# Linear-attention queries sketched like keys, and the token routing moved into a scatter under the attention

## The chip, the cores and the metric

The kernel runs on one core of a Trainium2 chip. The metric is device time in microseconds (us) of one execution; lower is better. TensorE (PE) multiplies matrices into PSUM, VectorE (DVE) and ScalarE (ACT) read PSUM and SBUF, GpSimd (POOL) here does a few elementwise operations and issues the indirect DMAs, SyncE (SP) issues the direct ones. Each engine runs its own instructions in order.

## The reference

```python
# attention: q, k, v are (4, 4, 1088, 32), S1 and S2 are (8, 32)
def phi(x):
    a = np.einsum('rd,bhsd->bhsr', S1, x)
    b = np.einsum('rd,bhsd->bhsr', S2, x)
    return np.einsum('bhsi,bhsj->bhsij', a, b).reshape(*x.shape[:-1], r * r)
q_p, k_p = (phi(q), phi(k))
kv = np.einsum('bhsf,bhsd->bhfd', k_p, v)
z = np.sum(k_p, axis=2)
num = np.einsum('bhsf,bhfd->bhsd', q_p, kv)
den = np.einsum('bhsf,bhf->bhs', q_p, z)[..., None] + 1e-06
x = (num / den)                      # then (B, H, S, D) -> (B*S, H*D) = (4352, 128)
# router over E = 8 experts, one expert for each token
xn = x / (np.linalg.norm(x, axis=-1, keepdims=True) + 1e-06)
en = expert_emb / (np.linalg.norm(expert_emb, axis=-1, keepdims=True) + 1e-06)
logits = xn @ en.T / tau
expert_idx = np.argmax(logits, axis=1)
gate_w = probs[np.arange(N), expert_idx]           # probs: softmax of logits over the experts
for e in range(E):
    mask = expert_idx == e
    h = np.maximum(x[mask] @ w1[e], 0.0)               # w1[e] is 128 x 1024
    out[mask] = gate_w[mask, None] * (h @ w2[e])       # w2[e] is 1024 x 128
```

All arrays are float32 (S1 and S2 arrive as 64-bit words).

## The kernel before

The four batches are handled as two halves `m` (2176 tokens each, 17 columns of 128 tokens). Keys of a half go through `k_steps` in groups of four columns: `tr` transposes four tiles on TensorE, `ab` multiplies them with the block matrix `Sblk` (96 columns wide) to get both sketches of all heads, VectorE forms the 64 products of each head (L276), and `kv` accumulates features times `[v, v, 1]` for pairs of heads (L288, 128 outputs by 96 columns, of which the cross terms are masked away with `maskh`).

Queries (`q_steps`) run otherwise. After the transposes, `fa` and `fb` multiply the transposed group with `Sa` and `Sb`, which repeat each sketch row eight times, so that the 64 features of a head come out already transposed (L328, two matmuls of 512 columns each); ScalarE copies one (L335), VectorE multiplies the two (L340). `nd` gives numerator and denominator (L348), with the 64 tokens of each batch written to their own half of the PSUM partitions; VectorE divides (L354 to L356). `xt` transposes x again, ScalarE sums squares (L367), and `logit` multiplies with the normalized expert rows, padded to 96 columns (L372).

The order of steps is given by ticks: `put(tick, steps)` lays the steps of one group on consecutive ticks, and the second half's keys share ticks with the first half's queries. Up to there the framework's scheduler may still reorder; `route_and_run_experts` alone is under a manual schedule of VectorE and TensorE.

Routing begins when all logits are there. `pick` finds the expert of each token, two matmuls (L418, L419) count and rank tokens, `gate_tokens` takes the norm with GpSimd's power (L399), multiplies x by the gate (L408, GpSimd) and stores x to `x_dram` (L410). VectorE then works out each token's slot in a list of 41 blocks of 128 tokens (each block has one expert), builds one-hot rows (L462 to L466), and 34 small matmuls (L469) invert the list into token numbers `src_i` and `dst_i` and an expert number for each block.

The expert loop runs 41 blocks. `fetch(i)` gathers 128 rows of x by an indirect DMA (four blocks ahead), `turn(i)` transposes them, `weights(i)` copies the expert's w1 and w2 with VectorE by a register, `up(i)` is eight matmuls and a Relu on ScalarE, `down(i)` is eight matmuls, a copy on ScalarE and an indirect DMA that scatters the rows to `out`.

Of the kernel before, what the change touches and what calls it, by code (L numbers as in the profile page):

```python
# [19 lines left out]
P = 128  # L20
B, H, S, D = 4, 4, 1088, 32
R = 8
# [11 lines left out]
K_GROUPS = ((0, 4), (4, 8), (8, 12), (12, 16), (16, 17))  # L34
Q_GROUPS = ((0, 4), (4, 8), (8, 11), (11, 14), (14, 17))
# [3 lines left out]
NOWHERE = 8192.0  # L39
DIGIT = 128  # L40
# [9 lines left out]
def kernel(  # L50
# [28 lines left out]
    def ps_acc(i):  # L79
        return psum.tile([P, 512], F32, tag=f"acc{i}", bufs=1, name=f"ps_acc{i}")  # L80
# [6 lines left out]
    def rows_tile(name):  # L87
        return rows_p.tile([P, NC, H, D], F32, tag="rows", name=name)

    def load_q(m):  # L90

        for i in range(2):
            for h in range(H):
                nc.sync.dma_start(
                    q_sb[m][i * HALF:(i + 1) * HALF, :, h],
                    bass.AP(tensor=q.tensor, offset=q.offset + ((2 * m + i) * H + h) * S * D,
                            ap=[[NC * D, HALF], [D, NC], [1, D]]))


    v_sb = [consts.tile([P, 6, NC, D], F32, name=f"v{m}") for m in range(NM)]  # L100

    def load_k(m, i):
        for h in range(H):
            nc.sync.dma_start(
                k_sb[m][:, i * NK:(i + 1) * NK, h],
                bass.AP(tensor=k.tensor, offset=k.offset + ((2 * m + i) * H + h) * S * D,
                        ap=[[NK * D, P], [D, NK], [1, D]]))

    def load_v(m, i):
        for p in range(2):  # L110
            nc.sync.dma_start(
                v_sb[m][:, 3 * p:3 * p + 2, i * NK:(i + 1) * NK],
                bass.AP(tensor=v.tensor, offset=v.offset + ((2 * m + i) * H + 2 * p) * S * D,
                        ap=[[NK * D, P], [S * D, 2], [1, NK * D]]))

    def load_rest(m):
        for i in range(2):
            r = slice(i * HALF, (i + 1) * HALF)
            at = (2 * m + i) * H * S * D + SK * D
            nc.sync.dma_start(k_sb[m][r, NC - 1],  # L120
                              bass.AP(tensor=k.tensor, offset=k.offset + at, ap=[[D, HALF], [S * D, H], [1, D]]))
            for p in range(2):
                nc.sync.dma_start(v_sb[m][r, 3 * p:3 * p + 2, NC - 1],
                                  bass.AP(tensor=v.tensor, offset=v.offset + at + 2 * p * S * D,
                                          ap=[[D, HALF], [S * D, 2], [1, D]]))
# [4 lines left out]
    for m in range(NM):  # L130
        k_sb[m] = rows_tile(f"k{m}")
# [4 lines left out]
        q_sb[m] = rows_tile(f"q{m}")  # L136
# [13 lines left out]
    for m in range(NM):  # L150
        for p in range(2):
            nc.gpsimd.memset(v_sb[m][:, 3 * p + 2], 1.0)

    mask4 = consts.tile([P, H], F32, name="mask4")
    maskh = consts.tile([P, 2], F32, name="maskh")
    for t in (mask4, maskh):
        nc.vector.memset(t, 0.0)
    for h in range(H):
        nc.vector.memset(mask4[h * D:(h + 1) * D, h:h + 1], 1.0)
    for h in range(2):  # L160
        nc.vector.memset(maskh[HALF * h:HALF * (h + 1), h:h + 1], 1.0)
# [28 lines left out]
    nc.vector.tensor_copy(ST, ps[:, :2 * R])  # L190

    Sblk = consts.tile([P, 6, 2 * R], F32, name="Sblk")
    nc.vector.memset(Sblk, 0.0)
    nc.vector.tensor_mul(Sblk[:, :H], bview(ST, [[0, H], [1, 2 * R]]), bview(mask4, [[1, H], [0, 2 * R]]))
    Sa = consts.tile([P, H, R, R], F32, name="Sa")
    Sb = consts.tile([P, H, R, R], F32, name="Sb")
    for h in range(H):
        nc.vector.tensor_scalar_mul(Sa[:, h], bview(ST, [[1, R], [0, R]]), mask4[:, h:h + 1])
# [410 lines left out]
```

## Time and profile before

| | |
|---|---|
| median of 3 runs | 310.73 us (309.41 to 311.48) |
| profiled execution | 309.62 us |
| its span, first to last instruction | 307.8 us |
| mean granted TensorE clock | 0.916 |
| TensorE busy | 254.5 us (83%) |
| VectorE, ScalarE, GpSimd busy | 140.1, 86.5, 107.2 us |
| DMA | 22.59 MB in 51194 packets, 38425 of them under 512 bytes |

Times in the profile are counted from the start of the span. A group's line names the code line, the engine, the operation, output and inputs with shapes, then busy time and the mean of one in ns, then the idle time of that engine just before and what ended it. PEld is TensorE's loading of weights. An fp32 matmul is recorded as two matmul instructions, a transpose as one.

### The profile page before, as it was taken

The page shows a single profiled execution, that of the slowest core. Times are in us where ns is not written, and L with a number is a line of the kernel's source. Part 1 is how long each engine was busy: PE and PEld are TensorE (multiplying, and loading weights), DVE is VectorE, ACT ScalarE, POOL GpSimd, SP SyncE. Part 2 cuts the span into 40 slices and gives each one's busy share as a digit, 9 for nine tenths or more (in the row PEclk, how much of TensorE's full clock was granted, in tenths as well). Part 3 has the DMA queues.
Part 4 walks back from the last instruction along what each step waited for, and adds up shares of the span by engine and source line. Part 5 has one row for each costly group of instructions (what it writes and reads, how often), then busy time and mean ns, then how long its engine had stood idle before and what let it go on. Part 6 is the DMA issues. An engine that isn't in the chain of part 4 may idle for free. (4 is left out here: it accounts for less than half of the span.)

```text
span 307.8 us, 5515 instructions
## 1 busy us (share of the span) xinstructions
PE 254.5 (83%) x2127; PEld 230.3 (75%) x2127; DVE 140.1 (46%) x345; ACT 86.5 (28%) x195; POOL 107.2 (35%) x103
## 2 busy tenths in 40 slices
PE   0987999999799750125999999999999999999960
PEld 0886777776467530114999999999999999999960
DVE  7334254345464448982344444444444444444400
ACT  1121242332245210001133333333333333333320
POOL 4000000000413034017455666555666556632230
PEclk9999799999999955555799999999999999999995
DMA  6999799993003001102111111111111111210000
GB/s 122 167 136 171 146 135 327 336 345 85 0 2 145 1 2 66 79 0 48 30 34 38 34 37 28 36 30 44 37 30 37 34 40 32 36 25 19 15 2 0
DMA packets 51194, 22.59 MB, mean 73 GB/s; under 512 B 38425, under 2 KB 48676, under 8 KB 50912
## 3 DMA queue, kind: packets, MB, share of 16 engines
q1 hardware_dynamic: 48544, 17.31, 24.2%
q0 software_dynamic: 2624, 4.92, 6.2%
q8 instruction: 17, 0.28, 0.4%
q14 instruction: 9, 0.07, 0.1%
HBM read 17.77 MB, written 4.92 MB: 74 GB/s over the span
## 5 line engine op out<-in xcount | busy, mean ns | idle before, releaser
L522 PE MATMUL ps_big<-xTb,w1b 128*128 128x128 f32 x656 | 83.6, 283 | 1.7 <-issue 1.3
L522 PEld LDWEIGHTS ps_big<-xTb,w1b 128*128 128x128 f32 x656 | 79.8, 199 | 2.4 <-issue 1.7
L529 PE MATMUL ps_acc<-w2b,hT 128*128 128x128 f32 x656 | 79.8, 275 | 0.0
L529 PEld LDWEIGHTS ps_acc<-w2b,hT 128*128 128x128 f32 x656 | 76.4, 192 | 0.0
L523 ACT ACTIVATE hT<-ps_big 128x1024 f32<-128x1024 f32 x41 | 42.1, 1027 | 94.6 <-PE ps_big L522 83.6
L497 POOL DMA_INDIRECT xs<-x_dram,src_i x41 | 48.0, 1170 | 39.4 <-PE ps_t L503 21.4
L532 POOL DMA_INDIRECT out_dram<-y,dst_i x41 | 41.4, 1010 | 50.3 <-ACT y L531 48.4
L505 DVE COPY xTb<-ps_t 128x128 f32<-128x128 f32 x41 | 12.0, 292 | 75.0 <-PE ps_t L503 75.0
L512 DVE COPY w1b<-w_sb 128x1024 f32 x41 | 28.5, 694 | 13.5 <-DVE xTb L505 12.1
L399 POOL TENSOR_TENSOR nrm<-ssq,half_c 128x17 f32<-128x17 f32 x2 | 6.2, 3087 | 65.7 <-ACT sq L367 65.7
L513 DVE COPY w2b<-w_sb 128x1024 f32 x41 | 28.5, 694 | 0.0
L340 DVE TENSOR_TENSOR qp<-a_sb,ps_big 128x768 f32<-128x768 f32 (+1 forms) x10 | 10.6, 1055 | 23.4 <-PE ps_big L328 20.3
L531 ACT COPY y<-ps_acc 128x128 f32<-128x128 f32 x41 | 11.0, 267 | 33.9 <-PE ps_acc L529 33.9
L288 PE MATMUL ps_acc<-v,kp 128*128 128x96 f32 (+1 forms) x144 | 19.8, 295 | 0.8 <-DVE kp L276 0.8
L288 PEld LDWEIGHTS ps_acc<-v,kp 128*128 128x128 f32 (+1 forms) x144 | 18.2, 206 | 2.9 <-DVE kp L276 1.6
L276 DVE TENSOR_TENSOR kp<-ps_t,b_sb 128x256 f32<-128x256 f32 x34 | 12.1, 418 | 14.5 <-ACT b_sb L272 14.5
L469 PE MATMUL ps_acc<-col,row 128*128 128x82 bf16 x34 | 3.0, 269 | 18.3 <-DVE row L466 18.3
L328 PE MATMUL ps_big<-qT,Sa 128*128 128x384 f32 (+1 forms) x40 | 17.3, 556 | 0.0
L367 ACT ACTIVATE sq<-x 128x128 f32<-128x128 f32 x34 | 10.3, 308 | 24.2 <-DVE x L356 24.2
L469 PEld LDWEIGHTS <-row 128*128 128x128 bf16 x34 | 2.3, 138 | 19.7 <-DVE row L466 19.7
L328 PE MATMUL ps_big<-qT,Sb 128*128 128x384 f32 (+1 forms) x40 | 16.5, 534 | 0.0
L503 PE MATMUL ps_t<-ident,xs 128*128 128x128 f32 x41 | 11.5, 281 | 4.2 <-DMA xs<-x_dram,src_i 4.2
(137 smaller groups left out, 220.3 us busy)
## 6 DMA issues: line engine op xcount, KB each, us to landing
w_sb<-in_moe_w_dram SPq DMA_DIRECT2D x16, 512.0 KB, 8.3
q<-in_q_dram SPq DMA_DIRECT2D x16, 136.0 KB, 4.2
x_dram<-x SPq DMA_DIRECT2D x2, 1088.0 KB
k<-in_k_dram SPq DMA_DIRECT2D x16, 128.0 KB, 3.8
v<-in_v_dram SPq DMA_DIRECT2D x8, 256.0 KB, 3.3
xs<-x_dram,src_i POOLq DMA_INDIRECT x41
out_dram<-y,dst_i POOLq DMA_INDIRECT x41
k<-in_k_dram SPq DMA_DIRECT2D x4, 32.0 KB, 3.4
```

The source lines that it names most:

```text
L276: nc.vector.tensor_mul(s["kp"][:, j], bview(a, [list(a.ap[1]), list(a.ap[2]), [0, R]]), bview(b, [list(b.ap[1]), [0, R], list(b.ap[2])]))
L288: nc.tensor.matmul(acc[m][i][:, p], s["kp"][r, c - c0, 2 * p:2 * p + 2].rearrange("s h i j -> s (h i j)"), v_sb[m][r, 3 * p:3 * p + 3, c], ...
L328: nc.tensor.matmul(ps[:, p, :w], S_[:, 2 * p:2 * p + 2].rearrange("p h i j -> p (h i j)"), s["qT"][:, :w], start=True, stop=True)
L497: nc.gpsimd.indirect_dma_start(out=xs[i][:], out_offset=None, in_=x_dram[:, :], in_offset=bass.IndirectOffsetOnAxis(ap=src_i[:, i:i + 1], ...
L503: nc.tensor.transpose(ps[:, :P], xs.pop(i), ident)
L505: nc.vector.tensor_copy(xT[i], ps[:, :P])
L512: nc.vector.tensor_copy(w1b[i], w1_sb[:, bass.ds(e, 1)].rearrange("p o f -> p (o f)"))
L513: nc.vector.tensor_copy(w2b[i], w2_sb[:, bass.ds(e, 1)].rearrange("p o f d -> p (o f) d"))
L522: nc.tensor.matmul(ps[:, u, j * P:(j + 1) * P], w[:, f * P:(f + 1) * P], x, start=True, stop=True)
L523: nc.scalar.activation(hT[i], ps, ACT.Relu)
L529: nc.tensor.matmul(ps, h[:, f * P:(f + 1) * P], w[:, f], start=f == 0, stop=f == NF - 1)
L532: nc.gpsimd.indirect_dma_start(out=out[:, :], out_offset=bass.IndirectOffsetOnAxis(ap=dst_i[:, i:i + 1], axis=0), in_=y[:], in_offset=None ...
```

## The change

Loads. k, q and v are loaded with whole rows of several tokens at a time (`[[NK * D, P], [S * D, H], [1, NK * D]]`), one DMA for each batch, so k and q tiles now hold heads outside and tokens inside. The last column of each half comes from extra tiles `k_rest` and `q_rest`.

Attention. One function pair serves keys and queries: `turned` transposes, `sketch` multiplies tokens (as 64-wide weights, one half of PSUM partitions for each batch) with `Sblk`, `features` forms products on VectorE in one instruction of 1024 columns for each group. Queries then transpose their features (`tr_qp`, eight transposes, ScalarE's copy of 1024 columns). `kv` multiplies each head alone, 64 outputs by 64 columns. `logit` multiplies 64 tokens at a time with 8 expert columns.

Routing. x is kept in groups of eight columns together with its shifted logits, its sum of squares and its token number, a row of 138 words. When eight columns are there, `router` picks the expert, ranks the tokens with two bf16 matmuls, continuing the counts of the group before, and `place` scatters the rows by indirect DMAs, 128 rows each, to regions of `rows` in DRAM, one region of 4352 rows for each expert. That makes 17 scatters for each half. Scatters are declared to have no row in common with each other, with early fetches and so on (`apart`).

Blocks. After the first half's scatters, `table_early` takes ten full blocks from it; they can begin while the second half's queries still run. `table_late` lists the other 31. A block's rows bring their logits and squares along: `norm` takes the power on GpSimd (one column) for each block, ScalarE takes Exp with its sum, `share` the reciprocal, and the gate is applied when `y` is copied out of PSUM.

Order. All steps of TensorE, VectorE and ScalarE are now in one manual order: by tick, and inside a tick by a rank. GpSimd and SyncE are left to the scheduler. A key or query group starts every second tick; the keys of the first half start at tick 0, the mixed groups at tick 10, the second half's queries at tick 20, and block `i` stands in tick 29 + i.

```diff
-K_GROUPS = ((0, 4), (4, 8), (8, 12), (12, 16), (16, 17))
-Q_GROUPS = ((0, 4), (4, 8), (8, 11), (11, 14), (14, 17))
+GROUPS = ((0, 4), (4, 8), (8, 12), (12, 16), (16, 17))
+SPAN = 8
+ROW = DM + E + 2
...
+EARLY = (NM * NC * P // 2 - E * (P - 1) + P - 1) // P
+LATE = NBLK - EARLY
...
+        nc.sync.dma_start(
+            k_sb[m][:, :, i].rearrange("p h c d -> p h (c d)"),
+            bass.AP(tensor=k.tensor, offset=k.offset + (2 * m + i) * H * S * D,
+                    ap=[[NK * D, P], [S * D, H], [1, NK * D]]))
...
+    def apart(dma, own, *others):
+
+        for group in others:
+            tc.declare_no_dep(dma.ins, group=group, reason="no row in common")
+        for group in own:
+            tc.add_to_no_dep_group(group, dma.ins)
+    apart(nc.gpsimd.dma_start(rows[E * N:], none.bitcast(I32)), ["rows"])
 
...
+        ps = ps_small()
+        if n == 1:
+            nc.tensor.transpose(ps[:, :P], rest.rearrange("p h d -> p (h d)"), ident)
+        else:
+            for h in range(H):
+                nc.tensor.transpose(ps[:, h * P:(h + 1) * P], tiles[:, h].rearrange("p c d -> p (c d)"), ident)
+        t = work.tile([P, 512], F32, tag=tag, name=tag)
+        nc.scalar.copy(t[:, :n * P], ps[:, :n * P])
+        return t
...
+    def sketch(ps, t, n):
+
+        for u in range(2):
+            r = slice(u * HALF, (u + 1) * HALF)
+            if n == 1:
+                nc.tensor.matmul(ps[r, :H * 2 * R], t[:, r], Sblk.rearrange("p g r -> p (g r)"), start=True, stop=True)
+            else:
+                for h in range(H):
+                    nc.tensor.matmul(ps[r].rearrange("p (g h r) -> p g h r", h=H, r=2 * R)[:, :, h],
+                                     t[:, h * P + u * HALF:h * P + (u + 1) * HALF], Sblk, start=True, stop=True)
+        return ps[:, :n * H * 2 * R].rearrange("p (g t r) -> p g t r", t=2, r=R)
...
+    def features(ab, b, n, tag):
+        t = work.tile([P, 4, H, R * R], F32, tag=tag, name=tag)
+        nc.vector.tensor_mul(t[:, :n].rearrange("p j h (i k) -> p (j h) i k", i=R),
+                             ab[:, :, 0].unsqueeze(3).broadcast_to([P, n * H, R, R]),
+                             b[:, :n * H].unsqueeze(2).broadcast_to([P, n * H, R, R]))
+        return t
...
+                        for u in range(2):
+                            h = 2 * p + u
+                            vo = v_sb[m][r, h, c]
+                            own = acc[m][:, i] if not rest or i == 0 else end
+                            nc.tensor.matmul(
+                                own[u * HALF:(u + 1) * HALF, p], s["kp"][r, c - c0, h],
+                                bass.AP(tensor=vo.tensor, offset=vo.offset,
+                                        ap=[list(vo.ap[0]), [(H - h) * NC * D, 2], [1, D]]),
+                                start=p == 0 and (c == 0 or own is end), stop=rest, skip_group_check=True)
...
+        put(0, 60, tr)
+        put(1, 51, ab)
+        put(1, 61, b)
+        put(1, 63, prod)
+        put(5 if late else 3, 30, kv)
...
+        def tr_qp():
+            ps = ps_big()
             for j in range(n):
+                for p in range(2):
+                    nc.tensor.transpose(ps[:, p, j * P:(j + 1) * P],
+                                        s["qp"][:, j, 2 * p:2 * p + 2].rearrange("p h f -> p (h f)"), ident)
+            s["qpT"] = work.tile([P, 2, 512], F32, tag="qpT", name="qpT")
+            nc.scalar.copy(s["qpT"][:, :, :w], ps[:, :, :w])
...
+        put(0, 61, tr)
+        put(1, 50, ab)
+        put(1, 60, b)
+        put(1, 62, prod)
+        put(3, 10, tr_qp)
+        put(4, 20, nd)
+        put(5, 20, xt)
+        put(5, 80, squares)
+        put(6, 10, logit)
+        put(6, 70, best)
+        if c1 == NC or c1 % SPAN == 0:
+            pick, place = router(m, c1 - at - n, c1)
+            put(6, 71, pick)
+            put(7, 40, place)
...
+        def place():
+
+            oh = s["oh"][:, :, 1:]
+            ps = ps_small()[:, :E * n].rearrange("p (e j) -> p e j", e=E)
+            nc.tensor.matmul(ps, before, oh, start=True, stop=False)
+            nc.tensor.matmul(ps, ones, s["cum"][:, :, :n], start=False, stop=True)
+            t = work.tile([P, SPAN, E], F32, tag="lt", name="lt")[:, :n]
+            f = work.tile([P, SPAN], F32, tag="mx8", name="mx8")[:, :n]
+            nc.vector.tensor_mul(t, ps.rearrange("p e j -> p j e"), oh.rearrange("p e j -> p j e"))
+            nc.vector.reduce_sum(out=f, in_=t, axis=AX.X)
+            slot = work.tile([P, SPAN], I32, tag="slot", name="slot")
+            nc.vector.tensor_scalar_add(slot[:, :n], f, float(E // 2 * N))
             for j in range(n):
+                d = nc.gpsimd.indirect_dma_start(
+                    out=rows[:, :], out_offset=bass.IndirectOffsetOnAxis(ap=slot[:, j:j + 1], axis=0),
+                    in_=xg[m, c0 // SPAN].bitcast(I32)[:, j], in_offset=None)
+
+                if m == 0:
+                    apart(d, ["rows"], "rows")
+                else:
+                    apart(d, ["rows", "rows1"], "rows", "early")
...
+    def table_early():
+
+        ps = ps_small()[:, :E]
+        nc.tensor.matmul(ps, ones, counts[0], start=True, stop=True)
+        ni, full, upto, w = column("n_early", I32), column("full"), column("upto0"), column("w_early")
+        nc.vector.tensor_sub(ni, ps, region)
+        nc.vector.tensor_scalar(ni, ni, 7, None, op0=ALU.logical_shift_right)
+        nc.vector.tensor_copy(full, ni)
+        nc.vector.tensor_tensor_scan(out=upto[:], data0=ones[:, :E], data1=full[:], initial=0.0, op0=ALU.mult, op1=ALU.add)
+        nc.vector.tensor_scalar(w, full, -float(P), float(N), op0=ALU.mult, op1=ALU.add)
...
+    def fetch(i):
+        t, j = of(i)
+        xs[i] = work.tile([P, ROW], F32, tag="xs", bufs=AHEAD + 3, name="xs")
+        d = nc.gpsimd.indirect_dma_start(
+            out=xs[i].bitcast(I32)[:], out_offset=None, in_=rows[:, :],
+            in_offset=bass.IndirectOffsetOnAxis(ap=src[t][:, j:j + 1], axis=0))
+        if t == 0:
+            apart(d, ["early"], "rows1")
...
+    def norm(i):
+        rn[i] = work.tile([P, 1], F32, tag="rn", bufs=3, name="rn")
+        nc.gpsimd.tensor_tensor(out=rn[i], in0=xs[i][:, DM + E:DM + E + 1], in1=half_c, op=ALU.pow)
+        nc.vector.tensor_scalar_add(rn[i], rn[i], NORM_EPS)
+        nc.vector.reciprocal(rn[i], rn[i])
...
+        p = work.tile([P, E], F32, tag="probs", name="probs")
+        gate[i] = work.tile([P, 1], F32, tag="gate", bufs=3, name="gate")
+        nc.scalar.activation(p, xs[i][:, DM:DM + E], ACT.Exp, scale=rn.pop(i)[:, 0:1], accum_out=gate[i])
...
+    def share(i):
+        nc.vector.tensor_scalar_add(gate[i], gate[i], PROB_EPS)
+        nc.vector.reciprocal(gate[i], gate[i])
...
+        y = work.tile([P, DM], F32, tag="y", bufs=3, name="y")
+        nc.scalar.activation(y, ps, ACT.Copy, scale=gate.pop(i)[:, 0:1])
+        x = xs.pop(i)
+        d = nc.gpsimd.indirect_dma_start(
+            out=out[:, :], out_offset=bass.IndirectOffsetOnAxis(ap=x.bitcast(I32)[:, ROW - 1:], axis=0),
+            in_=y[:], in_offset=None, bounds_check=N - 1, oob_is_err=False)
+        apart(d, ["out"], "out")
...
+    def first_block():
         for i in range(AHEAD):
             fetch(i)
+        norm(0)
         weights(0)
         turn(0)
...
+    def block(i):
+
+
+        if i + AHEAD < NBLK:
+            fetch(i + AHEAD)
+        if i < NBLK:
+            up(i)
+        if i + 1 < NBLK:
+            turn(i + 1)
+            weights(i + 1)
+        if i < NBLK:
+            share(i)
+        if i + 1 < NBLK:
+            norm(i + 1)
+        if i > 0:
+            down(i - 1)
+
...
+    for g in GROUPS:
+        keys(0, *g, put_at(tick), True)
         tick += 2
-    put(tick + 4, [lambda: pick(0), lambda: gate_tokens(0)])
-    for g in Q_GROUPS:
-        put(tick, q_steps(1, *g))
+    put_at(tick)(0, 0, prep_emb)
+    for g in GROUPS:
+        keys(1, *g, put_at(tick), False)
+        queries(0, *g, put_at(tick))
         tick += 2
-    for i in sorted(at):
-        for f in at[i]:
-            f()
-
-    with tc.manual_schedule(engines={mybir.EngineType.DVE, mybir.EngineType.PE}):
-        route_and_run_experts()
+    put_at(tick)(5, 90, table_early)
+    put_at(tick)(8, 90, first_block)
+    for g in GROUPS:
+        queries(1, *g, put_at(tick))
+        tick += 2
+    put_at(tick)(5, 50, table_late)
+    for i in range(NBLK + 1):
+        put_at(tick)(i - 1, 55, lambda i=i: block(i))
+
+    with tc.manual_schedule(engines={mybir.EngineType.PE, mybir.EngineType.DVE, mybir.EngineType.Activation}):
+        for i in sorted(at):
+            ps = None
+            for _, _, f in sorted(at[i], key=lambda x: x[:2]):
+                if f.__name__ == "ab":
+                    if ps is None:
+                        ps = ps_one("ab")
+                    f(ps)
+                else:
...
+                    f()
```

## The prediction

> **What bounds the kernel now.** I read the page's forty slices first, then the busy time by stages, the groups of instructions, and last the timeline for pitches.
>
> ```profile
> PE   0987999999799750125999999999999999999960
> DVE  7334254345464448982344444444444444444400
> PEclk9999799999999955555799999999999999999995
> 110.00:120.00 10.00, 2.28 (x5) 1.18 (x4) 7.51 (x20) 0.32 (x1) 4.90 (x2) 0.50 0.01 2
> 120.00:130.00 10.00, 0.79 (x9) 0.61 (x9) 9.52 (x20) 0.00 (x0) 1.21 (x1) 0.50 0.27 111
> 140.00:150.00 10.00, 7.76 (x33) 7.09 (x34) 2.67 (x6) 1.02 (x1) 6.22 (x7) 0.50 0.19 46
> 150.00:285.00 135.00, 135.00 (x1211) 135.00 (x1210) 59.05 (x111) 47.68 (x74) 75.92 (x69) 1.00 0.13 33
> ```
>
> The columns of a stage are its length, then busy time of PE, PEld, DVE, ACT and POOL, the granted clock, and DMA. TensorE sets the time twice: until 110, and without a gap from 150 on. Between them it idles while VectorE works through the routing, and the clock falls to 0.50 until about 150. By the timeline the 307.8 us are: first key transpose at 7.3; attention to 110.1 (102.8); routing until the first expert matmul at 141.4 (31.3); experts to 297.6 (156.2); tail 10.2. In steady state a block starts every 3.68 us (288.41 to 292.09), and 41 x 3.68 = 151, so the slow clock cost 5.
>
> ```profile
> 82.92 1.07 PEld L348 LDWEIGHTS ps_big<-kz,qp 128*64 128x64 f32 x32 [2.10 <-DVE qp L340]
> 84.06 1.98 PE L328 MATMUL ps_big<-qT,Sa 128*128 128x512 f32 x4
> 85.88 0.60 PE L362 MATMUL ps_t<-ident,x 128*128 128x128 f32 x4
> 88.26 0.97 PEld L372 LDWEIGHTS ps_t<-enT,xT 128*128 128x128 f32 x8
> 292.09 1.95 PE L522 MATMUL ps_big<-xTb,w1b 128*128 128x128 f32 x16
> ```
>
> These give prices per record (an fp32 matmul is two records, a transpose one): (0.60 - 0.27)/3 = 0.11 for a transpose, (1.95 - 0.28)/15 = 0.11 for a full 128-wide matmul, (0.97 - 0.20)/7 = 0.11 for the 96 columns, 0.43 for 512 columns (the loads between them start at 84.60 and 85.03), and only (1.07 - 0.14)/31 = 0.03 where the output is 64 wide and halves take turns; TensorE's own 32 records beside these loads took 1.21 with a last one of 0.22, which is 0.032, and that I use.
>
> **The change, part by part: TensorE in the attention.** Per four columns, keys now cost 4 transposes (0.44), 8 records against Sblk (0.86) and 16 of L288 (1.7): 3.0. Queries cost 0.44, twice 1.72 for Sa and Sb, 32 records of L348 (1.03), 0.44, 8 of L372 (0.86): 6.2. With 17 columns in each half, 8.5 x 9.2 = 78. After: keys 0.44, sketch 16 records at 0.032 (0.51), kv 32 (1.02): 1.97. Queries 0.44, sketch 0.51, eight transposes of the features (0.88), nd 1.03, 0.44, logits 16 (0.51): 3.81. Together 8.5 x 5.78 = 49. Lower bound: this. Upper: a 64-wide record costs half of 0.11, which adds 80 x 0.021 x 8.5 = 14. L348 is the same form, so I take 49, and 2 for changes of form: after a run of L348 the next 128-wide matmul starts some 0.12 late, before it some 0.08, and ranks put the 64-wide steps together, one run in two ticks. Sum 51.
>
> **Other time in the attention.** Before, 102.8 - 78 = 25 was not matmul pitch: loading, slow clock, handshakes. SP issued the second q's last piece only at 43, as 128-byte pieces cost it 0.8 us each; rows of 1 KB, like v's at 0.6 us, bring all q, k, v by about 25 and the weights by 50, before anything needs them. What stays: five key groups, each a chain of sketch 0.5, b 0.3 and one 1024-wide product 1.2 (L340's row) with handshakes, 2.4 us, so keys end near 20 (5 over pitch); 4 for the slow clock (before, matmuls ran at half pitch until 16); 0.75 in each mixed group where x waits behind two products on VectorE. 12, with bounds 8 and 25. Start 6.5.
>
> **Routing.** The 31 us and the 5 of slow clock go; they become table_early, table_late and 34 scatters, laid under attention and early blocks. GpSimd carries them, and it is nowhere in the hand-made order.
>
> ```profile
> L497 POOL DMA_INDIRECT xs<-x_dram,src_i x33 | 39.4, 1195 | 21.1 <-PE ps_t L503 21.1
> L532 POOL DMA_INDIRECT out_dram<-y,dst_i x36 | 36.5, 1014 | 38.0 <-ACT y L531 38.0
> L399 POOL TENSOR_TENSOR nrm<-ssq,half_c 128x17 f32<-128x17 f32 x2 | 6.2, 3087 | 65.7 <-ACT sq L367 65.7
> L242 POOL TENSOR_TENSOR emb_ss<-emb_ss,half_c 8x1 f32<-8x1 f32 x1 | 0.6, 575 | 18.3 <-ACT emb_sq L241 18.3
> ```
>
> Unhindered fetches follow each other every 1.25 us (0.95 and 0.3 of gap). A scatter is bounded by 0.94 and 1.5, the extremes of L497, plus the gap; I take 1.25 with it. The ticks: keys to 20, then 4.25 groups of 6.7 to 49, then 4.2 us for two ticks. The places of the first half fall into ticks 19, 23 and 25, near 46, 55 and 60; GpSimd ends its 17 scatters near 66, the last lands 2 later, and fetch 0 needs 3.2 to its transpose (137.39 to 140.56 before): 72, where tick 28 is reached at 67. Stall 4.5. Tick 29: eight scatters stand before fetch 4 and the power of block 1. GpSimd, busy to 73.5 with four fetches, ends them at 84 and the power at 86. VectorE waits for that power in norm(1), and behind it stand the divisions of nd, the next turn and weights, so TensorE stops some 6. Tick 33 does the same with the next eight: 6.5. In tick 35 table_late is some 22 small operations of 0.2 on VectorE ahead of turn and weights, and fetch 10 holds the next power back: 4. Sum 21, bounds 0 (if the powers go ahead of the scatters) and 35. Such stops also cool the clock: after the 1.6 us without matmuls at 28.3 the same eight records of L270 took 2.02 instead of 1.13. I add 4, bounds 0 and 8.
>
> The Trainium skill, TensorE: Matmul & The Clock Gate, Why this matters for your kernels, has the clock fall only after gaps of about 3 us. In this trace 1.6 us were enough, so the shorter stops count too. By the page the three stops over 3 us alone would count, each followed by an estimated 3.4 us at half pace, 5 in all instead of my 4.
>
> The Trainium skill, SBUF — State Buffer, the section on the bandwidth-pool intuition, says that a GpSimd DMA of 620 ns took 3100 beside a VectorE copy, because descriptors can't be written. Here fetches take 1.195 beside two copies per block and 0.95 without, so the measurement decides; by the page's figure the 17 scatters of the second half would cost an estimated 17 x 1.9 = 32 us more.
>
> **Experts.** TensorE keeps its 17 operations a block: 151. Other engines must stay under 3.68. VectorE: 0.29 + 2 x 0.69 + four one-column operations of some 0.15 + a register load, 2.6. ScalarE: 1.03 + 0.27 + Exp and its accumulator read, 0.5: 1.8; the one table load of the page already served Exp, Relu, Copy and Square. GpSimd: fetch 1.195, out 1.014, two gaps of 0.3, and the new power. That is bounded by L242 (8x1, 0.575) and L399 (128x17, 3.087); one column is nearest L242, so 0.58 and a gap, and the block is 3.49. It fits by 0.2. gate_tokens' multiplications and both stores of x go; they were on the routing path counted above.
>
> **Tail.** The last out waited 1.3 for the one before it (297.97 to 299.29); outs are now declared apart: 9.
>
> **Sum.** 6.5 + 51 + 12 + 151 + 21 + 4 + 9 = 254.5 us of span. The profiled execution took 309.62 for a span of 307.8, and the median of the runs lies 1.1 above it, so 254.5 + 1.8 + 1.1 = 257.
>
> **Rivals.**
> Smooth: the scheduler lets powers and fetches pass the scatters, and the stops vanish with their cooling: 257 - 17 - 4 = 236. For it: GpSimd's order is free and VectorE is half idle. Against it: scatters are ready first and stand earlier in the program. 0.25.
>
> GpSimd bound: the power costs 0.9 beside VectorE's copies, fetch and out 0.1 more each, so a block takes 4.0: 34 x 0.32 = 11 more, 268. For it: only 0.2 us of room, and L497 rose from 0.95 to 1.195 beside copies. 0.18.
>
> The declarations don't hold, each scatter waits until the last has landed: the last two outs of the profile start 2.88 apart (296.41, 299.29). The first half's 17 take 49, which puts the first transpose at 98 instead of 72, and each eight of the second half 23 instead of 10: 257 + 26 + 26 = 309, no gain. Against it: the change names the groups explicitly. 0.04.
>
> On the other side: the power costs its 3.09 whatever its width. A GpSimd block is then 2.81 + 3.09 + 0.1 = 6.0, 41 x 2.3 = 95 more, 352. It decides from 5.0 a block, a power of 2.1 us, where 41 x 1.3 eats the whole gain of 53. For it: the only row on 128 partitions is that one. Against it: the 8x1 row of 0.575. 0.05.
>
> **Chances.** My forecast 0.48, and the predicted time is its 257. Faster by over 1%: forecast, smooth, GpSimd bound and half of the failed declarations, 0.93; within 1% the other half, 0.02; slower by over 1% the dear power, 0.05 (1% is about what a measurement of this kernel can tell from no change). The range runs from the smooth case to the GpSimd-bound one with 14 for serial 64-wide records and 4 for the cooling at its bound: 236 to 286.
>
> **What would show it.** Right: no stage of TensorE below half busy after 25 us; L348's form at 0.03 in sketch and kv; blocks 3.68 apart from tick 36 on; short gaps of TensorE near the eight-fold scatters with VectorE waiting for GpSimd's power. Wrong: blocks over 3.8 apart, powers over 0.9, scatters over 1.5 apart, or first expert matmul later than 80.

## The result, and the profile after

The changed kernel is slower: 328.8 us median against 310.07 for the kernel before, ratio 1.053, 95% interval 1.040 to 1.067. The forecast was 257. The profiled execution took 327.49 us for a span of 325.7 (on a chip that the record doesn't name).

From the page after, the slices (tenths of busy time of TensorE, VectorE and GpSimd, and the granted clock):

```profile
PE   2967897474556889757599997867687787867785
DVE  5344458153525335534655544242434434243450
POOL 5000002717381735577465546455564645556484
PEclk9999999858595569797799999999999999999999
```

The hole of the routing is gone, but TensorE has nowhere the unbroken row of nines that it had from 150 on, and between 60 and 130 it is often half idle at a low clock. Two stages (length; busy time of PE, PEld, DVE, ACT and POOL; clock; DMA), one of the attention and the steady experts:

```profile
60.00:65.00 5.00, 1.60 (x12) 1.21 (x12) 0.74 (x3) 0.00 (x0) 3.85 (x4) 0.72 0.17 57
...
165.00:300.00 135.00, 109.32 (x940) 106.10 (x939) 56.74 (x194) 50.10 (x113) 74.63 (x78) 1.00 0.09 25
```

The steady stage held 1,211 matmul records in 135 us before, now 940: from 193 on blocks start 5.16 us apart (208.52, 213.68, 218.83) instead of 3.68. The groups that answer to those shown of before:

```profile
L571 POOL DMA_INDIRECT xs<-rows_dram,src x41 | 40.3, 982 | 71.2 <-DMA out_dram<-y,xs 36.5
L482 POOL DMA_INDIRECT rows_dram<-xg,slot x34 | 33.8, 994 | 58.6 <-ACT sq L409 33.5
...
L624 POOL DMA_INDIRECT out_dram<-y,xs x41 | 50.5, 1232 | 10.3 <-issue 7.2
...
L594 POOL TENSOR_TENSOR rn<-xs,half_c 128x1 f32<-128x1 f32 x41 | 25.7, 628 | 8.3 <-ACT probs L610 7.4
```

The operations together cost about what was forecast: the fetch takes 0.98 (1.195 forecast), the power 0.63 (0.58), the output 1.23 (1.014, the one that is clearly dearer), 2.84 for the three where the sum had 2.79; the scatter takes 0.99 with 0.3 of gap. New is what the fetch waits for: the landing of an output write. The longest waits of the run, in all, times, longest:

```profile
DVE rn L595 <- POOL rn L594: 69.6, 25, 3.4
ACT y L622 <- DMA out_dram<-y,xs: 48.7, 24, 2.5
POOL xs L571 <- DMA out_dram<-y,xs: 36.5, 18, 2.1
```

GpSimd's timeline in the steady state (start, duration, wait before) shows the loop:

```profile
207.15 1.34 POOL L624 DMA_INDIRECT out_dram<-y,xs  x1 [0.19 <-issue]
210.53 0.98 POOL L571 DMA_INDIRECT xs<-rows_dram,src  x1 [2.04 <-DMA out_dram<-y,xs]
211.53 0.59 POOL L594 TENSOR_TENSOR rn<-xs,half_c 128x1 f32<-128x1 f32 x1
212.30 1.35 POOL L624 DMA_INDIRECT out_dram<-y,xs  x1 [0.19 <-issue]
215.69 0.97 POOL L571 DMA_INDIRECT xs<-rows_dram,src  x1 [2.04 <-DMA out_dram<-y,xs]
```

GpSimd isn't among the engines whose order is written by hand; the scheduler of the framework orders its queue. Counted in the trace, the fetch of block 21 stands directly behind the output of block 14, and so on: with seven xs tiles the fetch of block k takes the tile of block k-7, so the scheduler, as it seems, puts it in as soon as it thinks that tile free. There it waits 2.04 for that write to land, the next power and output wait behind it, and the output of the block after is as late again. 0.97 + 0.59 + 1.35 + 2.04 with two gaps is the 5.16. The loop is there from 164 on (outputs at 164.3, 169.2, 174.8); from 163 to 193 TensorE still started a block every 3.68, on rows and powers that GpSimd had got ready ahead.

A second thing is in the attention. TensorE's timeline, in a stretch where nothing in the program makes it wait:

```profile
62.23 0.49 PE L388 MATMUL ps_big<-kz,qpT 128*64 128x66 f32 x3 [1.11 <-issue]
63.67 0.61 PE L388 MATMUL ps_big<-kz,qpT 128*64 128x66 f32 x4 [0.95 <-issue]
65.10 1.10 PE L271 MATMUL ps_t<-ident,q 128*128 128x128 f32 x4 [0.82 <-issue]
```

Three or four matmuls come every 1.43 us, where 32 of this form take 1.2 in the kernel before. Such stretches, in which TensorE issues little though nothing that the profile shows holds it (starved, for short), lie at 58.9 to 65.9, 93.9 to 98 and 111.7 to 117.8, each while GpSimd issues scatters or fetches about 1.27 us apart. Two more bursts of eight scatters, from 72 and from 138, show the loss in another form (below). The first expert matmul starts at 104.8.

### The profile page after: what moved, and what is told of

It is laid out like the page before. It is cut to its first block, busy times and chain, and to the rows that moved or that the text cites. A ratio compares the mean times of both kernels' runs of the same rounds, so it can differ in the third digit from the quotient of the medians.

```text
span 325.7 us, 6593 instructions
## 1 busy us (share of the span) xinstructions
PE 243.0 (75%) x2507; PEld 227.4 (70%) x2507; DVE 141.3 (43%) x492; ACT 111.2 (34%) x305; POOL 155.4 (48%) x186
## 4 chain that ended last, share of the span: by engine, by line
PE 28%; DMA 23%; POOL 16%; DVE 13%; issue 13%; another core or an unknown queue 2%; ACT 1%; POOLq 1%; SPq 1%; DVEq 1%; ACTq 0%
DMA out_dram<-y,xs 17%; PE ps_big L605 12%; POOL xs L571 10%; POOL rn L594 5%; PE ps_acc L620 3%; DVE qp L295 3%; DMA q<-in_q_dram 2%; PE ps_ab L284 2%; PE ps_ab L620 2%; PE ps_acc L331 2%; PE ps_big L388 2%; DMA k<-in_k_dram 2%; DMA k_rest<-in_k_dram 2%; DVE xg L396 1%
## 5 line engine op out<-in xcount | busy, mean ns | idle before, releaser
L571 POOL DMA_INDIRECT xs<-rows_dram,src x41 | 40.3, 982 | 71.2 <-DMA out_dram<-y,xs 36.5
L482 POOL DMA_INDIRECT rows_dram<-xg,slot x34 | 33.8, 994 | 58.6 <-ACT sq L409 33.5
L606 ACT ACTIVATE hT<-ps_big 128x1024 f32<-128x1024 f32 x41 | 42.0, 1024 | 57.1 <-PE ps_big L605 27.4
L624 POOL DMA_INDIRECT out_dram<-y,xs x41 | 50.5, 1232 | 10.3 <-issue 7.2
L620 PE MATMUL ps_acc<-w2b,hT 128*128 128x128 f32 x336 | 41.8, 279 | 0.0
L620 PEld LDWEIGHTS ps_acc<-w2b,hT 128*128 128x128 f32 x336 | 40.2, 196 | 0.0
L620 PE MATMUL ps_ab<-w2b,hT 128*128 128x128 f32 x320 | 39.3, 276 | 0.0
L620 PEld LDWEIGHTS ps_ab<-w2b,hT 128*128 128x128 f32 x320 | 37.7, 194 | 0.0
L595 DVE TENSOR_SCALAR rn<-rn 128x1 f32<-128x1 f32 x41 | 6.0, 146 | 69.6 <-POOL rn L594 69.6
L594 POOL TENSOR_TENSOR rn<-xs,half_c 128x1 f32<-128x1 f32 x41 | 25.7, 628 | 8.3 <-ACT probs L610 7.4
L388 PE MATMUL ps_big<-kz,qpT 128*64 128x66 f32 x272 | 15.2, 254 | 5.3 <-issue 5.3
L388 PEld LDWEIGHTS ps_big<-kz,qpT 128*64 128x64 f32 x272 | 13.4, 163 | 5.8 <-issue 5.6
```

The lines of the kernel that those rows point to most:

```text
L388: nc.tensor.matmul(ps[i * HALF:(i + 1) * HALF, j, p * W:(p + 1) * W], s["qpT"][:, p, j * P + i * HALF:j * P + (i + 1) * HALF], kz[m][:, i, ...
L482: d = nc.gpsimd.indirect_dma_start(out=rows[:, :], out_offset=bass.IndirectOffsetOnAxis(ap=slot[:, j:j + 1], axis=0), in_=xg[m, c0 // SPAN ...
L571: d = nc.gpsimd.indirect_dma_start(out=xs[i].bitcast(I32)[:], out_offset=None, in_=rows[:, :], in_offset=bass.IndirectOffsetOnAxis(ap=src[ ...
L594: nc.gpsimd.tensor_tensor(out=rn[i], in0=xs[i][:, DM + E:DM + E + 1], in1=half_c, op=ALU.pow)
L606: nc.scalar.activation(hT[i], ps, ACT.Relu)
L620: nc.tensor.matmul(ps, h[:, f * P:(f + 1) * P], w[:, f], start=f == 0, stop=f == NF - 1)
```

## The experiments

Theory: the two losses are GpSimd's order (the loop over the landing) and the late, starved start. Rivals: too few buffers, GpSimd's raw work, VectorE's wait for the power. Runs fell on four chips, called A to D here. The kernel before takes 307 to 313 on all of them, but the changed kernel doesn't (below), so experiments are compared on one chip. A time without a range is that of a single run; four runs of one kernel, the paced one, lay between 264.4 and 268.8.

**Buffers alone** (chip A).

```
-        xs[i] = work.tile([P, ROW], F32, tag="xs", bufs=AHEAD + 3, name="xs")
+        xs[i] = work.tile([P, ROW], F32, tag="xs", bufs=AHEAD + 8, name="xs")
...
-        y = work.tile([P, DM], F32, tag="y", bufs=3, name="y")
+        y = work.tile([P, DM], F32, tag="y", bufs=8, name="y")
```

> Fetched rows get twelve buffers instead of seven, expert outputs eight instead of three; nothing else. Theory (order on GpSimd): the scheduler lets a fetch go ahead as soon as its buffer is free, so with twelve buffers it stands eight blocks ahead and again waits for the landing of the output write issued just before it. The loop fetch 0.97 + power 0.59 + output 1.35 + landing 2.04 stays, so blocks stay 5.1 to 5.2 us apart and the time at 322 to 330. ScalarE's waits for free y buffers (48.7 us in all) vanish without bringing anything. Rival (too few buffers): the waits are what they are called, blocks come 3.7 to 4.0 apart and the time falls to about 328 - 31 x 1.3 = 288.

299.7 us. The time is far under the 322 to 330, because chip A has no starved stretches (below): the changed kernel itself takes 304.3 there. The period is mostly as expected, 5.15 to 5.2 from block 13 to block 34, with the fetch still waiting for a landing:

```profile
181.18 1.35 POOL L624 DMA_INDIRECT out_dram<-y,xs  x1 [0.19 <-issue]
184.62 0.97 POOL L571 DMA_INDIRECT xs<-rows_dram,src  x1 [2.10 <-PE ps_big L605]
```

(The 2.10 is put down to a matmul; by the count of the queue, the tile that the fetch wants is that of the output issued just before it, now twelve blocks back.) Five more tiles moved the loop, they did not open it. The last seven blocks, for which all rows are fetched, come 3.68 apart, and there lies all that this run gains on the changed kernel, 4.6 us.

**A pace for the fetches** (chip A), with the twelve and eight buffers.

```
+        ix = src[t][:, j:j + 1]
+        if i >= AHEAD:
+            ix = work.tile([P, 1], I32, tag="ix", bufs=AHEAD, name="ix")
+            nc.vector.tensor_copy(ix, src[t][:, j:j + 1])
...
-            in_offset=bass.IndirectOffsetOnAxis(ap=src[t][:, j:j + 1], axis=0))
+            in_offset=bass.IndirectOffsetOnAxis(ap=ix, axis=0))
```

> The same twelve and eight buffers, and each fetch from the fifth on reads its row numbers from a one-column copy that VectorE makes in the block four ahead of it, so that the scheduler can't put it earlier; GpSimd's order becomes fetch of i+4, power of i+3, output of i-1. Theory (order): the loop over the landing is open, GpSimd has 3.5 us of work in a block, blocks come 3.7 to 3.9 apart from the table of late blocks on: 328 - 31 x 1.35 = 286, 278 to 295. Rival (GpSimd's raw work or VectorE's wait for the power sets the block): 4.3 or more, over 300. The first expert matmul stays near 105 in either.

264.6 us, 3.68 a block from 135 to the end. That is under the 278 to 295, which was reckoned from 328; the same step from the 304.3 of this chip gives 262. Its second run:

> The paced kernel with twelve and eight buffers once more, nothing altered. Beside the first paced run (264.6, no stretches of starved TensorE) stand two close relatives from another chip (pace_only 292.6, paced_xg 291.1), both with such stretches between 59 and 118. If the stretches come with the program (its buffers, the place of its instructions), this one has none again and takes 262 to 268; if they come with the chip or the execution, it may show them and take 288 to 294, and then the third run of the changed kernel, sent with it, shows them too.

266.4 median of four, ratio 0.863 (0.855 to 0.872) to the kernel before. From its stages and GpSimd's timeline:

```profile
140.00:250.00 110.00, 109.99 (x986) 109.83 (x985) 63.05 (x237) 50.15 (x120) 90.16 (x89) 1.00 0.14 37
```

```profile
181.35 1.19 POOL L575 DMA_INDIRECT xs<-rows_dram,ix  x1 [0.30 <-issue]
182.57 0.89 POOL L598 TENSOR_TENSOR rn<-xs,half_c 128x1 f32<-128x1 f32 x1
183.68 1.05 POOL L628 DMA_INDIRECT out_dram<-y,xs  x1 [0.22 <-DVE ix L573]
```

TensorE is busy without a gap again. GpSimd has 1.19 + 0.89 + 1.05 and 0.55 of gaps in a block, 3.68: it keeps up, with little to spare. The wait of VectorE for the power, 69.6 in the changed kernel, is 4.0 in all.

**The pace alone**, with seven and three buffers (chip B).

> The one-column copy that holds each fetch to its block, with the changed kernel's own seven and three buffers. Theory (order alone): fetch i+4 needs the output of i-3 landed, which GpSimd issued two blocks earlier, so nothing waits for a landing; blocks 3.68 apart as with twelve buffers, time 262 to 270. Rival (order and buffers are both needed): ScalarE waits for y buffers or GpSimd for fetched rows' buffers again, blocks 4.2 or more apart, 280 or more.

292.6 us, outside 262 to 270, but with blocks 3.68 apart, as the theory said; what is too much lies before 160, in stretches of starved TensorE. On the same chip the changed kernel took 326.4, so order is worth 34 there. Buffers add nothing that shows: the same chip took 291.1 with twelve and eight (and a tile for each group of columns, below).

**The power out of the block** (chip A): the norm is taken in pick and travels in the row; norm(i) and its calls go.

```
+            nr = xg[m, c0 // SPAN][:, :n, DM + E]
+            nc.gpsimd.tensor_tensor(out=nr, in0=nr, in1=half_c.broadcast_to([P, n]), op=ALU.pow)
+            nc.vector.tensor_scalar_add(nr, nr, NORM_EPS)
+            nc.vector.reciprocal(nr, nr)
...
-        nc.scalar.activation(p, xs[i][:, DM:DM + E], ACT.Exp, scale=rn.pop(i)[:, 0:1], accum_out=gate[i])
+        nc.scalar.activation(p, xs[i][:, DM:DM + E], ACT.Exp, scale=xs[i][:, DM + E:DM + E + 1], accum_out=gate[i])
```

> The norm (power, plus epsilon, reciprocal) is taken once for a group of eight columns before the scatter and travels in the row, so a block has no power on GpSimd and no wait of VectorE for it; buffers and order as in the changed kernel. Theory (order): the loop loses only the power: 0.97 + 1.35 + 2.04 = 4.4 with its gap, blocks 4.4 to 4.6 apart, 328 - 31 x 0.7 = 306, 300 to 312. Rival (VectorE's wait for the power, 69.6 us in all, is what the block pays): 3.7 apart, 283.

298.0 us, 2 under the 300 to 312, again reckoned from 328 and not from the chip's 304.3: blocks are 3.68 apart for longer, until 212, and then 3.7 to 5.5, 4.6 in the mean (sixteen blocks from 212.4 to 286.4). GpSimd's loop turns at 4.3 long before that (fetches at 157.8, 162.1, 166.4, each after a wait of 2.0); until 212 TensorE lives on what was fetched ahead. So the blocks stay slow without any power in them, and the rival (VectorE's wait for it is the price) falls. The power of eight columns takes 1.68, one column 0.63; it stands behind eight scatters in the queue, so the first expert matmul is late, at 103.7 instead of 92.5.

**Experts after the attention** (chip A).

```
-    put_at(tick)(8, 90, first_block)
+    put_at(tick)(18, 90, first_block)
...
-        put_at(tick)(i - 1, 55, lambda i=i: block(i))
+        put_at(tick)(i - 1 + 10, 55, lambda i=i: block(i))
```

> All blocks, the ten early ones too, start ten ticks later, after the last attention tick; nothing else. Theory: early blocks bring next to nothing, as they run at 5 us or more under starved or waiting engines: attention then ends near 90 to 95, the first expert matmul stands at about 105 to 110 and 41 blocks at 5.16 follow, 212 + 9: 326 to 332. It also shows attention alone; before, it ended at 110. Rival (early blocks do fill the gaps): the first expert matmul is as late but nothing has been done under the attention, so 6 to 8 blocks, 25 to 40 us, come on top: 350 to 365.

314.0 us, 9.7 over the changed kernel on that chip. Attention ends near 94 (110 in the kernel before), the first expert matmul is at 110.5. Theory and rival were both wrong in size: the early blocks bring 10, neither nothing nor 25 to 40.

**The changed kernel again** (chip B, A and C).

> The changed kernel once more, nothing altered. In its first profile TensorE issued only one to four instructions every 0.72 or 1.43 us in three stretches (58.9 to 65.9, 93.9 to 98, 111.7 to 117.8) with no wait shown; the paced kernel has the same instructions up to there and no such stretch. If the stretches belong to this program they come again in the same places and the time is again 326 to 330; if they are a matter of the single execution they lie elsewhere or are gone, and the first expert matmul comes near 96 to 100 instead of 104.8.

> The changed kernel a third time, nothing altered, on the same chip as the second paced run. Stretches by the program: 325 to 330 with stretches, whatever the paced kernel does. Stretches by the chip: both kernels have them (325 to 330) or neither (about 328 - 25 = 303, first expert matmul near 92).

326.4 on chip B with the stretches in the same places, 304.3 on A without any, and 330.2 on C with them, some 3 us later (after_fourth; nothing altered). The first expert matmul is at 104.3 on B and 92.5 on A. So the stretches do not come with the program alone. A had none on two occasions; B and C were tried on one each, so a passing state of those two isn't excluded. The same five microseconds on A as shown above:

```profile
60.00:65.00 5.00, 3.96 (x70) 3.27 (x71) 4.17 (x15) 3.56 (x14) 3.78 (x5) 1.00 0.18 57
```

70 matmul records instead of 12, while GpSimd issues the same scatters.

The stretches are not the whole of it. In the bursts from 72 and from 138 TensorE's records mostly keep their usual pace, but engines that wait for it go on late. In the first run the last matmul of an accumulation ends at 143.07, and ScalarE copies the result at 151.05, after a wait for which the profile finds no releaser ("remote"):

```profile
141.12 1.95 PE L620 MATMUL ps_acc<-w2b,hT 128*128 128x128 f32 x16
151.05 0.37 ACT L622 ACTIVATE y<-ps_acc,gate 128x128 f32<-128x128 f32 x1 [7.27 <-remote]
```

On A it does so at once:

```profile
120.57 1.95 PE L620 MATMUL ps_acc<-w2b,hT 128*128 128x128 f32 x16
122.55 0.37 ACT L622 ACTIVATE y<-ps_acc,gate 128x128 f32<-128x128 f32 x1 [0.53 <-PE ps_acc L620]
```

Waits without a releaser add up to 31 us over VectorE and ScalarE in the first run. All six profiles with stretches have them, and no other has any but for one of 0.9 (pad_256, below).

**Spacing the scatters.** First on chip A, a GpSimd copy of 128x512 words, read by nobody, ahead of each scatter, on the paced kernel:

```
+                pad = work.tile([P, 512], I32, tag="pad", bufs=1, name="pad")
+                nc.gpsimd.tensor_copy(pad, slot[:, j:j + 1].broadcast_to([P, 512]))
```

> The paced kernel with a copy of 128x512 words on GpSimd ahead of every scatter, so that the 34 scatters start some 1.9 to 2.3 us apart instead of 1.27; the copies' output is read by nobody. If bursts of indirect transfers starve TensorE, stretches that the paced kernel shows in this batch are gone or halved here and the time is lower than its by 5 to 20; where the paced kernel shows none, the copies only delay fetch 0 by 17 x 0.8 = 14 and the time rises by 10 to 25. If something else starves TensorE, the stretches stay and the delay comes on top.

280.1 us against 266.4: on the calm chip only the delay. Then on chip C, beside the paced kernel with a tile for each group of query columns (paced_xg_timed, 293.1):

```
+                pad = work.tile([P, 192], I32, tag="pad", bufs=1, name="pad")
+                own = work.tile([P, 1], I32, tag="place", bufs=SPAN, name="place")
+                nc.gpsimd.tensor_copy(pad, slot[:, j:j + 1].broadcast_to([P, 192]))
...
+                nc.gpsimd.tensor_copy(own, pad[:, 0:1])
...
-                    out=rows[:, :], out_offset=bass.IndirectOffsetOnAxis(ap=slot[:, j:j + 1], axis=0),
+                    out=rows[:, :], out_offset=bass.IndirectOffsetOnAxis(ap=own, axis=0),
```

> The same with two GpSimd copies (128x192 and one column) ahead of every scatter, through which its row numbers go, so that scatters start about 1.8 us apart instead of 1.27. Theory (bursts starve TensorE where the chip does so): on such a chip the stretches shrink and the time is under 288; on a calm chip the copies only delay, 268 to 276. Rival (spacing has no influence): on a starving chip the stretches stay as long and the time is 295 or more.

> The same with five copies ahead of every scatter, so that scatters start about 2.7 us apart. Theory: near the spacing of the undeclared kernel (3.06, no stretch on the chip that had them), so no stretch anywhere; the delay of 34 x 1.4 costs on the calm chip 20 to 35, 281 to 296, and the same time on the starving chip, where it takes the stretches away. Rival (spacing has no influence): stretches stay on the starving chip, 310 or more.

290.7 and 332.0: neither lies where the theory had it, and the 332.0 lies where the rival had it. But the stretches are gone in both. Two stages without the copies on chip C:

```profile
60.00:65.00 5.00, 2.20 (x37) 2.00 (x35) 1.03 (x4) 0.23 (x1) 3.83 (x4) 0.96 0.18 57
65.00:70.00 5.00, 2.39 (x12) 1.51 (x10) 0.70 (x1) 1.00 (x7) 1.92 (x2) 0.50 0.12 42
```

and with them, on the same chip:

```profile
60.00:65.00 5.00, 4.26 (x72) 3.40 (x70) 3.41 (x12) 2.72 (x13) 3.31 (x8) 1.00 0.13 42
65.00:70.00 5.00, 3.73 (x54) 3.50 (x54) 3.24 (x8) 1.66 (x6) 3.83 (x7) 0.66 0.11 32
```

So on chip C bursts of indirect transfers 1.27 apart starve TensorE, and at 2.11 apart they don't (a single run, and another with 3.35); on B the kernel without declarations (below), 3.06 apart, has no stretch either. Spacing also leaves fewer transfers under way at once; the runs don't part the two. The gain went back into the delay: scatters ended at 94 instead of 77, so the first expert matmul came at 103.9, no earlier than with stretches (103.0). In the wide one scatters were 3.35 apart, not 2.7. Shorter gaps, on a fourth chip, D:

> Paced fetches, a tile for each group of query columns, the changed kernel's seven and three buffers, and one GpSimd copy of 128x256 words (read by nobody) ahead of every scatter: scatters about 1.5 us apart. Theory (short gaps already feed TensorE): no stretch on any chip, fetch 0 some 4 to 6 us later than without copies, 264 to 272, below the 293 that this kernel's twin took on a starving chip. Rival (only gaps near 1 us do it): on a starving chip stretches stay, 285 to 298; on the calm chip the two can't be told apart and the time is 264 to 272.

> The same with copies of 128x512 words, scatters 1.77 us apart. Theory: no stretch, 4 to 10 us above the kernel with the shorter copies, as scatters end later. Rival: on a starving chip below it, because only these gaps are long enough to feed TensorE.

274.6 (ratio 0.889, 0.881 to 0.898), over the 264 to 272, with scatters 1.56 apart, and 278.4 with 1.77; no stretch but two single waits of 0.7 in the former. Whether D starves TensorE at 1.27 wasn't tried, so this doesn't settle the spacing.

**No declarations** (chip B), on the paced kernel:

```
-        for group in others:
-            tc.declare_no_dep(dma.ins, group=group, reason="no row in common")
-        for group in own:
-            tc.add_to_no_dep_group(group, dma.ins)
+        pass
```

> The paced kernel with twelve and eight buffers, without any declaration that the indirect transfers touch no row in common. Theory (the declarations hold and matter): each scatter waits until the one before has landed, 3.2 to 3.6 apart instead of 1.27, so the 17 of the first half take 35 us more and those of the second half and the early fetches wait for one another too; 264 + 50 to 70 = 314 to 334. Rival (scatters and fetches would have overlapped the attention anyway): under 285.

313.7 us: scatters 3.06 apart (2.88 by the prediction's rival), the first expert matmul at 116, and no stretch. Against the paced kernel's span of 262.6, without stretches too but on chip A, the declarations are worth 311.9 - 262.6 = 49, if the chips don't differ otherwise.

**A tile for each group of columns.** On chip B beside pace_only, then on A beside the paced kernel:

```
-                xg[g] = work.tile([P, SPAN, ROW], F32, tag="xg", bufs=3, name="xg")
+                last = c0 == NC - 1
+                xg[g] = work.tile([P, 1 if last else SPAN, ROW], F32, tag="xg1" if last else "xg", bufs=2 if last else 4, name="xg")
```

> The paced kernel with twelve and eight buffers, and every group of eight query columns with a tile of its own (four of eight columns, two of one), so that the second half's x and token numbers wait for no scatter to land and no iota stands among the scatters on GpSimd. Theory (reuse of the tiles delays the transition): the iotas' waits of 1.4 and 1.1 us among the scatters go, the transposes of x at 74.6 lose their wait of 1.7, fetch 0 comes 2 to 4 us earlier than at 80.5, and the time is 259 to 263. Rival (the scatters themselves and the attention's pace set fetch 0): 264 to 266.

> The paced kernel with a tile of its own for each group of query columns, a second time, beside the paced kernel on the same chip. Theory: without the wait for the tiles it is 2 to 5 us below the paced kernel there, whatever the stretches do. Rival (the tiles' reuse costs nothing): within 1 us of it.

291.1 on B (pace_only 292.6), where stretches cover it, and 261.1 on A, 5 under the paced median and 3 under its lowest run: fetch 0 starts at 78.6 instead of 82.9. With an interval, on chip C:

> The paced kernel with a tile of its own for each group of query columns, unaltered, for its interval against the kernel before. On a chip where bursts of indirect transfers starve TensorE: 288 to 294, ratio 0.93 to 0.945; on one where they don't: 260 to 264, ratio 0.84 to 0.85.

293.1, ratio 0.941 (0.932 to 0.950). This version beats both kernels on every chip that it ran on.

## Why the prediction was wrong, point by point

The forecast was a gain, 257 us, and the kernel lost, 328.8. The sum was 254.5 of span and 325.7 came. The runs divide the 71.2: order of GpSimd 302.5 - 262.6 = 39.9 (changed kernel and paced kernel on chip A, with the larger buffers in the latter); starved TensorE 325.7 - 302.5 = 23.2 (the changed kernel where that occurs and on A; by the ninth block they are worth 163.48 - 136.74 = 26.7, of which some is regained later); the rest 262.6 - 254.5 = 8.1.

**The step that failed** is "Experts": "the block is 3.49. It fits by 0.2." As a sum of work it held: the paced kernel runs at 3.68, with the power at 0.58 to 0.89. But it priced GpSimd as if only work counted. It followed the program's order, fetch of i+4, power of i+1, output of i-1, although the prediction itself says that GpSimd "is nowhere in the hand-made order". What is put into the queue early is not free: a fetch that needs a buffer waits in place, here 2.04 for the landing of an output, and whatever is behind it waits too, so a block took 5.16. The prediction counted landings for scatters (a rival) and for the last output; no term or rival had a fetch wait for one. The slower outcome had got a chance of 0.05, for a dear power, which did not come.

**Missing altogether** was the starving of TensorE; nothing in the trace of before hinted at it, as its fetches were issued back to back (137.39 to 147.06) mostly while TensorE had nothing to do or had just begun.

**Stalls, 21**: on the paced kernel, where the order is mended, the first fetch's transpose waits 4.0 (4.5 forecast) and the table of late blocks costs 3.5 (4), while at ticks 29 and 33 (12.5) TensorE has no wait for a power, since the scheduler put three powers ahead of the scatters, as the smooth rival said. The two waits:

```profile
PE ps_t L583 <- DMA xs<-rows_dram,src: 4.0, 1, 4.0
PE ps_big L609 <- DVE w1b L593: 3.5, 1, 3.5
```

**Other time in the attention, 12**, was too small. On the paced kernel the first half's scatters start at 57 and not 46, and the first transpose is at 85, not 72. Keys ended near 21, as forecast; a mixed group took 7.1 and not 6.7, and I counted the group of the one last column as a quarter, while its chain of handshakes cost 5 us. In the sum: TensorE's waits between 78 and 136 add up to 13.4, 8 under the 21; what 6.5 + 51 + 151 + 9 and these leave of 262.6 is 32 for other time and cooled clock, 16 over the forecast's 12 + 4. 16 - 8 is the 8.1. So it is partly luck that the mended kernel, 264.6 to 266.4 on A, comes so near the 257: two terms were off by 16 and by 8 the other way.

**Right**: L388's form at 0.03 a record; power and scatter prices (0.63 for 0.58, 1.27 for 1.25); loads early enough; a cooled clock, though by less on the paced kernel (0.65 and 0.67 in the stages 70 to 75 and 75 to 80) than in the first run (0.72 in the stage from 60, and fives in the slices between 60 and 120), where the starving cooled it, which was not forecast; 49 for the declarations where the rival had 52. The prediction's other estimate for the cooling, 5, counts three stops over 3 us; its own sum has four (4.5, 6, 6.5 and 4), which makes that estimate 7. **Rivals**: the dear power fell (0.63). Of what would show the forecast wrong, two came: blocks over 3.8 apart, and the first expert matmul later than 80. Of what would show it right, the first failed: TensorE is 1.60 of 5.00 busy in the stage from 60.

## What to carry over

When some engines run in a hand-made order and one is left to a scheduler, read that engine's queue, instruction by instruction, before summing its work: an instruction that is issued early holds up all behind it until its buffer comes free. A cheap data dependency, here a one-column copy, paces such a queue without writing it by hand, while more buffers only move the wait. And where one engine's transfers can slow another, one chip may show it and the next not: run on more than one.

## What the runs showed of the hardware

Back-to-back indirect transfers from GpSimd, 1.27 us apart, slowed TensorE's issue to three or four matmuls every 1.43 us on chips B and C, and not at all on A, with the same program; in the same bursts a result of TensorE was read 8 us late. By the ninth block it cost 27 us (first run against A). At 2.11 apart they did not slow it on C, nor at 3.06 on B. What TensorE lacks in a stretch stays open. The Trainium skill, Runtime: NRT & Kernel Launch, Instruction fetch mechanics, has instructions arrive in blocks of 16 KiB, at a cost that is mostly hidden. The instruction queue's 20 packets with 0.33 MB agree on the size. None of them falls between 56 and 70, nor between 90 and 105 or 111 and 125, in the first run, so none of the three stretches ended with the landing of a block.

One power on GpSimd took 0.63 for 128x1 and 1.68 for 128x8.
